# Order alone: a planner that derives each operation's latest time from its own plan, and plans anew, three times

## The chip, the cores and the metric

One core of a Trainium2 chip runs the whole kernel. Time is microseconds (us) on the device, for one launch; smaller is better. The core's engines: TensorE (PE; its weight loads are shown as PEld), VectorE (DVE), ScalarE (ACT), GpSimd (POOL) and SyncE (SP), which here does nothing but issue DMA transfers.

## The reference, cut to what matters

Attention, then a feed-forward block, then a gated MLP, one into the next, all in float32 (the second and third block's weights come in 64 bits and are decoded in the kernel):

```
# B, H, S, D = 4, 12, 448, 64
s = 30 * tanh(q @ k.T / sqrt(D) / 30)                # softcap
x = softmax(s) @ v                                   # -> (4, 448, 768)
xn = (x - mean(x)) / sqrt(var(x) + 1e-6) * g_ln
x = x + relu(xn @ w_ch1) @ w_ch2                     # 768 -> 3072 -> 768
h = relu(x @ w_in)                                   # 768 -> 1024
u, v = h[..., :512], h[..., 512:]
v_s = w_spatial @ norm(v) + b_spatial                # over the 448 positions
out = (u * v_s) @ w_out                              # 512 -> 768
```

## The kernel before

The kernel's code does not issue instructions as it runs. Each call on an engine is *recorded* as an operation of a `Program`: its engine (or two or three alternatives, where `add`, `sub`, `cp` and the like allow several), a cost estimate, what it writes and reads, and the pooled buffers that it uses. A pooled buffer (`Buf`) gets a real tile of its pool (`Slots`) only when its first operation is planned, and gives it back when its last use is done. At the end `issue()` asks `order()` for a list of operations and emits it, so every instruction of the main part stands at one line of the profile, L553 (L588 after the change): one reads it by tile names, not by lines.

`order()` has two parts. The first gives each operation a number `due`. Matmul groups get the sum of the costs of the matmuls recorded ahead of them; everything else is traced backwards from its successors, at `SLACK` (0.35) of the costs in between. The second, `plan(due)`, is a list scheduler. It keeps a clock `now`, and whenever an engine is free it takes, among the engine's ready operations, the one with the smallest `due`, if tiles can be had for it and if that `due` is not further away than `reach()`. Before the change the reach is `spent + AHEAD`: matmul cost spent so far, plus 28. An operation with alternatives goes to its second or third engine only if the first would be later (`BIAS`). The plan decides three things: the order on each engine, which engine does an operation that has alternatives, and which tile a buffer gets.

The work in time. Attention fills about the first 105 us: scores into PSUM (`two`), softcap and exponential on ACT (`es`), with decoding of weights beside them. Decoded weights are stored in DRAM (`kept_w1_*`, `kept_w2_*`) for a second use, since the batch of four is worked in two halves. The feed-forward and gated stages follow in both halves, matmul after matmul. Their products are each three matmuls of a high and a low part (`rs`, `rx`, `rh`: activations; `wh`, `whb`, `whf`, `wab`: weights; a high part is a cast, a low part a subtraction), and blocks of 2x2 are combined in seven products instead of eight, with sums of tiles made on DVE. Hidden tiles of the feed-forward block go to DRAM (`h1_<product>_<tile> <- hs`, `<- hh`) and come back (`hs <- h1_..`). In the second half, kept w1 weights come through `wrb` to `whb`, two early w2 weights through `wr` to `wh`, and later w2 weights through `wq` to `wh`. A w1 or w2 weight serves six output tiles in the stages spoken of here, 3 matmuls each, so 18 matmuls of 448 columns. All transfers go through one queue, SP's, in the order of the plan.

```
cost, latency = 0.5, 4 * out.size() / 360e3      # a transfer, as the planner sees it
cost = 0.14 + n / 960                            # a DVE operation with two inputs
V.scalar_tensor_tensor(out=ti, in0=lo, scalar=29, in1=ti, op0=ALU.logical_shift_right, ...
SP.dma_start(out=kept2[j // KD][:, :, j % KD], in_=t.rearrange("p (a n) -> p a n", a=2))
```

The last two lines are the end of a weight's decoding (`value`): `wc` is the decoded tile, and storing it frees it for the next weight.

Of the kernel before, what the change touches and what calls it, by code (L numbers as in the profile page):

```python
# [44 lines left out]


AHEAD = 28
SLACK = 0.35
BIAS = 0.1
OPEN = 20.0  # L50
# [20 lines left out]
class View:  # L71


    def __init__(self, buf, ap, path=()):
        self.buf, self.at, self.path = buf, ap, path
# [25 lines left out]
class Buf:  # L101
    def __init__(self, pool, name):
        self.pool, self.name = pool, name
        self.first = self.last = None
        self.uses = self.left = 0
        self.tile = None
        self.after = []
        self.gates = []

# [39 lines left out]
class Slots:  # L149
# [19 lines left out]
            b.left, b.tile = b.uses, None  # L169

    def take(self, b):
        b.tile = self.idle.popleft()
        self.held.add(b)
        self.changes += 1

# [43 lines left out]
class Program:  # L219
# [102 lines left out]
    def order(self):  # L322
        n = len(self.ops)
        pred = self.edges()
        self.pred, self.succ = pred, [[] for _ in range(n)]
        for i, ds in enumerate(pred):
            for j, at in ds.items():
                self.succ[j].append((i, at))
        self.bufs = []
        for i, (_, writes, reads) in enumerate(self.ops):  # L330
            mine = list(dict.fromkeys(a.buf for a in chain(writes, reads) if isinstance(a, View)))
            for b in mine:
                b.first = i if b.first is None else b.first
                b.last = i
                b.uses += 1
            self.bufs.append(mine)
        self.pools = {b.pool for m in self.bufs for b in m}
        total = 0.0
        due = [float("inf")] * n
        for i in range(n):  # L340
            engine, cost = self.ops[i][0][0][:2]
            if engine == "PE":
                due[i] = total
                total += cost
            elif i in self.soon:
                due[i] = total
        for p in self.pools:
            p.reuse()
        for s in self.stages:
            begins = [b for p in s.pools for b in p.bufs if b.first is not None]  # L350
            if s.after and begins:
                first = min(begins, key=lambda b: b.first)
                for a in s.after:
                    for b in (b for p in a.pools for b in p.bufs if not b.after):
                        assert b.last < first.first
                        b.gates.append(first)
        for i in reversed(range(n)):
            engine, cost, latency = self.ops[i][0][0][:3]
            latency += 1.4 if engine == "D" else 0.0
            for j, at in chain(self.succ[i], {(a.first, 0.0) for b in self.bufs[i] for a in b.after},  # L360
                               {(a.first, -OPEN / SLACK) for b in self.bufs[i] for a in b.gates}):
                due[i] = min(due[i], due[j] + at * SLACK - (cost + latency + self.DELAY) * SLACK)
            if due[i] == float("inf"):
                due[i] = total
        for i in self.first:
            due[i] = float("-inf")
        return self.plan(due)

    def plan(self, due):

        n = len(self.ops)
        succ, bufs = self.succ, self.bufs
        for p in self.pools:
            p.reset()
# [4 lines left out]
        free = {e: 0.0 for e in self.engines}  # L379
# [5 lines left out]
        spent = moved = 0.0  # L385
        relief = float("-inf")
        blocked = {}

        def release(i):
            for k, alt in enumerate(self.ops[i][0]):  # L390
                heapq.heappush(ready[alt[0]], (due[i], i, k))
# [12 lines left out]
            return False  # L404

        def reach():
            return max(spent + AHEAD, relief)

        def pick(e):


            q = ready[e]
            skipped = []
            found = None
            while q and found is None:
                d, i, k = heapq.heappop(q)
                if taken[i]:
                    continue
                if d > reach():
                    skipped.append((d, i, k))  # L420
                    break
                if k:
                    alt = self.ops[i][0]
                    home = alt[0][0]
                    wait = max(0.0, free[home] - now) if busy[home] else 0.0
                    for d2, i2, k2 in ready[home]:
                        if not taken[i2] and (d2, i2) <= (d, i) and not k2:
                            wait += self.ops[i2][0][0][1]
                    if alt[k][1] > wait + BIAS:
                        skipped.append((d, i, k))  # L430
                        continue
                if not room(i):
                    skipped.append((d, i, k))
                    continue
                found = i, k
            for x in skipped:
                heapq.heappush(q, x)
            return found

        for i in range(n):  # L440
            if not left[i]:
                release(i)
        now = 0.0
        while True:
            for e in ready:
                if busy[e]:
                    continue
                found = pick(e)
                if found is None:
                    continue  # L450
                i, k = found
                taken[i] = True
                out.append((i, k))
                for b in bufs[i]:
                    if b.tile is None:
                        b.pool.take(b)
                busy[e] = True
                cost, latency = self.ops[i][0][k][1:3]
                if e == "PE":
                    spent += cost  # L460
                free[e] = now + cost
                if e == "D":
                    moved = max(moved, now + 1.5) + latency
                    latency = moved + 0.77 - now - cost
                heapq.heappush(events, (now + cost, 0, seq, e))
                done = now + cost + latency + self.DELAY
                for j, at in succ[i]:
                    heapq.heappush(events, (max(now, done - at), 1, seq, j))
                    seq += 1
                heapq.heappush(events, (done, 2, seq, i))  # L470
                seq += 1
            if not events:
                rest = [d for q in ready.values() for d, i, _ in q if not taken[i] and d > reach()]
                if not rest:
                    break
                relief = min(rest)
                continue
            relief = float("-inf")
            now, kind, _, x = heapq.heappop(events)
            if kind == 0:  # L480
                busy[x] = False
            elif kind == 1:
                left[x] -= 1
                if not left[x]:
                    release(x)
            else:
                for b in bufs[x]:
                    b.left -= 1
                    if not b.left:
                        b.pool.give(b)  # L490
                        if b.pool.stage is not None and not b.pool.stage.left:
                            for s in b.pool.stage.then:
                                if not s.open and all(not a.left for a in s.after):
                                    s.open = True
                                    out.append((s, None))
                                    for p in s.pools:
                                        p.changes += 1
        assert sum(k is not None for _, k in out) == n
        return out

# [1342 lines left out]
```

## Time and profile before

| | |
|---|---|
| runs shown | 1015.18, 1011.96, 1010.72 us; median 1011.96 |
| profiled execution | 1010.06 us; its span 1008.3 us, so 1.76 us lie around the span |
| granted TensorE clock | 1.000 over the span |
| TensorE matmul busy | 999.5 us, 99% of the span, 5060 matmuls |
| TensorE weight load busy | 828.4 us, 82% |
| DVE busy | 868.3 us, 86%, 1472 instructions |
| ACT busy | 580.5 us, 58%, 925 instructions |
| POOL busy | 23.0 us, 22 instructions |
| DMA | 229.05 MB, mean 227 GB/s |

An engine's busy time is the sum of its instructions' spans; matmuls overlap, so a busy TensorE is not a TensorE at its peak. What an instruction waited for is told by who released it. The waits of TensorE are what the span consists of beside its matmuls.

### The profile page before, as it was taken

The numbers are of one execution on the slowest core, as the hardware profiler recorded it, in microseconds if no ns is written. First come the engines' busy times: TensorE is split into PE (matmuls) and PEld (weight loads), VectorE is DVE, ScalarE is ACT, GpSimd is POOL, SyncE is SP. The second block draws the span as 40 slices with busy tenths as digits, with TensorE's granted clock in tenths as the row PEclk, the third lists the DMA queues.
The fourth block names the chain that finished last, engine by engine and source line by source line (L and its number), as shares of the span: only waits on it lengthen the run. The fifth ranks groups of instructions, "written<-read, shape, count | busy, mean of one in ns | idle before, by whom it ended". The sixth has DMA issues, their size and how long they took to land.

```text
span 1008.3 us, 14836 instructions
## 1 busy us (share of the span) xinstructions
PE 999.5 (99%) x5060; PEld 828.4 (82%) x5060; DVE 868.3 (86%) x1472; ACT 580.5 (58%) x925; POOL 23.0 (2%) x22
## 2 busy tenths in 40 slices
PE   9999999999999999999999999999999999999998
PEld 2332788778778899999989899999999999998987
DVE  6979898878888789999869999877788988968996
ACT  8999776776667347674335355444454542314653
POOL 0000110000000000000001200000000000000010
PEclk9999999999999999999999999999999999999999
DMA  8444779999999999998044143565699867302402
GB/s 282 136 128 146 261 262 366 357 365 356 343 368 361 362 376 323 330 405 276 26 154 141 39 138 122 176 194 191 232 330 375 291 183 233 103 22 71 128 22 110
DMA packets 124848, 229.05 MB, mean 227 GB/s; under 512 B 21170, under 2 KB 93028, under 8 KB 124772
## 3 DMA queue, kind: packets, MB, share of 16 engines
q1 hardware_dynamic: 124772, 228.10, 66.0%
q8 instruction: 40, 0.66, 0.3%
q14 instruction: 36, 0.29, 0.1%
HBM read 157.48 MB, written 70.57 MB: 226 GB/s over the span
## 4 chain that ended last, share of the span: by engine, by line
PE 78%; DMA 11%; DVE 6%; ACT 3%; issue 1%; SPq 1%; DVEq 0%; ACTq 0%
PE bank L553 51%; PE two L553 26%; DMA hs<-inv 3%; DMA w<-in_w_dram 3%; DVE es L553 2%; DMA kept_w<-wc 2%; DMA rc<-sum 1%; ACT es L553 1%; SPq L553 1%; DMA inv<-rc 1%; DVE wr L553 1%; DVE hs L553 1%; ACT hs L553 1%; DMA qk<-in_qk_dram 1%; DVE x L553 1%
## 5 line engine op out<-in xcount | busy, mean ns | idle before, releaser
L553 PE MATMUL bank<-rs,wh 128*128 128x448 f32 x1728 | 361.9, 363 | 0.3 <-ACT hs L553 0.2
L553 PEld LDWEIGHTS bank<-rs,wh 128*128 128x128 f32 x1728 | 322.8, 187 | 27.5 <-issue 4.3
L553 PE MATMUL two<-rs,wh 128*128 128x448 f32 x462 | 103.4, 362 | 0.0
L553 ACT ACTIVATE rs<-hs 128x448 fp32r<-128x448 f32 x137 | 74.6, 570 | 43.0 <-DMA hs<-h 33.2
L553 DVE TENSOR_TENSOR rs<-hs,rs 128x448 fp32r<-128x448 f32 x159 | 94.2, 618 | 1.8 <-ACT rs L553 1.4
L553 PEld LDWEIGHTS two<-rs,wh 128*128 128x128 f32 x462 | 86.6, 187 | 5.8
L553 ACT ACTIVATE es<-es,capt 128x896 f32<-128x896 f32 x72 | 73.1, 1057 | 0.0
L553 ACT ACTIVATE es<-two,qsc 128x896 f32<-128x896 f32 x62 | 60.7, 1017 | 6.8 <-PE two L553 6.6
L553 PE MATMUL bank<-es,vt 128*64 128x448 f32 x288 | 62.2, 552 | 0.0
L553 DVE TENSOR_TENSOR wh<-wr,wh 128x768 fp32r<-128x768 f32 (+2 forms) x66 | 56.3, 856 | 3.8 <-ACT wh L553 3.5
L553 ACT ACTIVATE hs<-bank 128x448 f32<-128x448 f32 x62 | 33.6, 541 | 44.6 <-PE bank L553 34.5
L553 ACT ACTIVATE wh<-wr 128x768 fp32r<-128x768 f32 (+2 forms) x50 | 38.5, 770 | 28.2 <-PE bank L553 15.3
L553 DVE TENSOR_TENSOR es<-es,es 128x896 f32<-128x896 f32 x48 | 51.9, 1081 | 1.8 <-ACT es L553 1.4
L553 PEld LDWEIGHTS bank<-es,vt 128*64 128x64 f32 x288 | 17.4, 136 | 36.9 <-issue 26.7
L553 PE MATMUL two<-qk 64*128 64x448 f32 x168 | 39.9, 580 | 2.0 <-ACT es L553 2.0
L553 ACT ACTIVATE wc<-w 128x512 f32<-128x512 f32 x36 | 24.2, 674 | 30.0 <-DMA kept_w<-wc 13.3
L553 ACT ACTIVATE rs<-x 128x448 fp32r<-128x448 f32 x32 | 18.0, 574 | 37.5 <-DVE x L553 36.1
L553 PEld LDWEIGHTS two<-qk 64*128 64x128 f32 x168 | 14.1, 190 | 27.3 <-ACT es L553 15.4
L553 PE MATMUL two<-wh,rs 128*128 128x512 f32 x144 | 34.7, 390 | 0.0
L553 PE MATMUL bank<-rx,whb 128*128 128x448 f32 x144 | 32.7, 362 | 0.0
L553 PE MATMUL two<-rx,whb 128*128 128x448 f32 x144 | 32.7, 362 | 0.0
L553 DVE TENSOR_SCALAR wc<-wc 128x512 int32<-128x512 int32 x36 | 15.2, 423 | 19.3 <-ACT wc L553 19.0
(249 smaller groups left out, 1878.9 us busy)
## 6 DMA issues: line engine op xcount, KB each, us to landing
hs<-h SPq DMA_DIRECT2D x168, 224.0 KB, 5.2
h<-hx SPq DMA_DIRECT2D x84, 224.0 KB, 5.3
w<-in_w_dram SPq DMA_DIRECT2D x24, 768.0 KB, 6.8
w<-in_w_dram SPq DMA_DIRECT2D x36, 512.0 KB, 6.4
qk<-in_qk_dram SPq DMA_DIRECT2D x24, 448.0 KB, 5.1
h<-hs SPq DMA_DIRECT2D x48, 224.0 KB, 3.7
kept_w<-wr SPq DMA_DIRECT2D x24, 384.0 KB, 7.6
kept_w<-wc SPq DMA_DIRECT2D x36, 256.0 KB, 5.3
```

Of the source, the lines that this page charges most:

```text
L553: fn(*(put(a) for a in args), **{k: put(a) for k, a in kw.items()})
```

## The change

The formula for `due` is kept as a first guess. With it the planner makes a plan as before. Then `latest()` goes through that plan from its end: an operation's latest time is the earliest of what its engine does next, of its successors, and of the next buffer that gets its tile, each less the lag seen in the plan, and less its cost. These times become the `due` of the next plan; for it, `reach()` is `now + WITHIN` (20), since `due` is now on the plan's own clock. That is done three times (`ROUNDS`); of the four plans the one with the smallest end by the planner's own costs is made again and issued. Nothing that is computed changes, and no operation is added or left out; what changes is order, choice of engine, and tiles.

```diff
+WITHIN = 20
+ROUNDS = 3
...
-        self.tile = None
+        self.tile = self.tile_at = None
...
-        b.tile = self.idle.popleft()
+        b.tile = b.tile_at = self.idle.popleft()
...
-        for i in self.first:
-            due[i] = float("-inf")
-        return self.plan(due)
-
-    def plan(self, due):
+        tries = []
+        for timed in (False,) + (True,) * ROUNDS:
+            for i in self.first:
+                due[i] = float("-inf")
+            plan = self.plan(due, timed)
+            tries.append((self.end, len(tries), due, timed))
+            due = self.latest(plan)
+        _, _, due, timed = min(tries)
+        return self.plan(due, timed)
+
+    def latest(self, plan):
...
+        late = [float("inf")] * len(self.ops)
+        free = {e: self.end for e in self.engines}
+        then = [[] for _ in self.ops]
+        users, holds = {}, {}
+        for i, k in plan:
+            if k is None:
+                continue
+            for b in self.bufs[i]:
+                t = id(b.tile_at)
+                if holds.get(t) is not b:
+                    for j in users.get(t, ()):
+                        then[j].append(i)
+                    holds[t], users[t] = b, []
+                users[t].append(i)
+        for i, k in sorted((x for x in plan if x[1] is not None), key=lambda x: -self.span[x[0]][0]):
+            e, cost = self.ops[i][0][k][:2]
+            lag = self.span[i][1] - self.span[i][0] - cost
+            t = min(chain([free[e]], (late[j] + at - lag for j, at in self.succ[i]), (late[j] - lag for j in then[i])))
+            late[i] = free[e] = t - cost
+        return late
+
+    def plan(self, due, timed):
...
-            return max(spent + AHEAD, relief)
+            return max(now + WITHIN if timed else spent + AHEAD, relief)
...
+                self.span[i] = now, done
...
+        self.end = now
```

TensorE's order is the same before and after, operation for operation. On the other engines operations move. Of those that may go to either engine, 70 casts and copies go from ACT to DVE and 59 from DVE to ACT, 2 operations go from POOL to DVE and 1 from DVE to POOL. The order listing has 1459 rows on DVE before and 1472 after, 927 and 916 on ACT, 27 and 26 on POOL, 833 and 836 on SP; some rows stand for several instructions. Three places follow.

The first is on SP, at the end of attention, before:

```order
L553 DMA vt1_0_423<-in_v_dram 64x2x64
L553 DMA w41_442<-in_w2_dram 128x1024
L553 DMA kept_w2_0_164<-wc1_440 256x1x256
L553 DMA vt1_0_423<-in_v_dram 128x2x192
L553 DMA qk0_420<-in_qk_dram 128x896
L553 DMA h0_1_0_168<-hx0_429 128x448
```

and after:

```order
L588 DMA vt1_0_423<-in_v_dram 64x2x64
L588 DMA w41_442<-in_w2_dram 128x1024
L588 DMA vt1_0_423<-in_v_dram 128x2x192
L588 DMA qk0_420<-in_qk_dram 128x896
L588 DMA kept_w2_0_164<-wc1_440 256x1x256
L588 DMA h0_1_0_168<-hx0_429 128x448
```

`wc0`, `wc1` are decoded w2 weights, `w41` a raw one, `vt1_0` and `qk0` are inputs of the last attention head, `hx0` a hidden tile. The store of `wc1` has moved behind two loads.

The second is on SP, in the second half of the batch, where the feed-forward block goes over from w1 to w2. Before:

```order
L553 DMA hs7_86<-h1_7_2_340 128x448
L553 DMA hs1_80<-h1_7_3_347 128x448
L553 DMA h1_1_11_398<-hh1_5133 128x448
L553 DMA hs4_83<-h1_7_4_354 128x448
L553 DMA wq0_6533<-kept_w2_12_209 128x768
L553 DMA wq1_6534<-kept_w2_18_223 128x768
L553 DMA h1_2_11_400<-hh5_5137 128x448
```

and after:

```order
L588 DMA hs8_87<-h1_7_3_347 128x448
L588 DMA h1_4_10_397<-hs7_86 128x448
L588 DMA hs2_81<-h1_7_4_354 128x448
L588 DMA h1_3_11_399<-hs9_88 128x448
L588 DMA hs5_84<-h1_7_5_361 128x448
L588 DMA hs1_80<-h1_7_6_368 128x448
L588 DMA hs3_82<-h1_7_7_375 128x448
L588 DMA h1_1_11_398<-hh3_5135 128x448
L588 DMA hs7_86<-h1_7_8_382 128x448
L588 DMA wq0_6543<-kept_w2_12_209 128x768
L588 DMA wq1_6544<-kept_w2_18_223 128x768
```

The rows `hs<-h1_7_n` load hidden tiles (operands of the seventh product), `h1_..<-hh` store some, and `wq0` is the first weight of the `wq` group. Ahead of `wq0` stand the loads of `h1_7_2` to `h1_7_4` before, and of `h1_7_2` to `h1_7_8` after: four more. In the same way, going back some 20 rows, the load of `kept_w1_21` to `wrb0` has no load of a `h1_1_n` tile ahead of it before and seven after, and one more of a weight (`kept_w2_6`); its place among the rows goes from 649 to 664.

The third is on DVE, near the end, where gated tiles are multiplied in. Before:

```order
L553 TENSOR_TENSOR x1_1_119<-x1_1_119,hs4_83 128x448
L553 TENSOR_TENSOR x1_2_120<-bank2_139,x0_5_117 128x448
L553 TENSOR_TENSOR hs2_81<-x1_1_119,x0_1_113 128x448
L553 TENSOR_TENSOR rc3_7732<-hs1_80,rc3_7732 128x448
L553 TENSOR_TENSOR x1_3_121<-two0_141,x0_5_117 128x448
L553 TENSOR_TENSOR rc0_7729<-hs2_81,rc0_7729 128x448
```

and after:

```order
L588 TENSOR_TENSOR x1_1_119<-x1_1_119,hs5_84 128x448
L588 TENSOR_TENSOR x1_2_120<-bank0_137,x0_5_117 128x448
L588 TENSOR_TENSOR hs0_79<-x1_1_119,x0_1_113 128x448
L588 TENSOR_TENSOR x1_2_120<-x1_2_120,hs6_85 128x448
L588 TENSOR_TENSOR rc3_7732<-hs4_83,rc3_7732 128x448
L588 TENSOR_TENSOR x1_3_121<-two0_141,x0_5_117 128x448
```

A multiplication that writes `x1_2` in place stands there now, the fourth row. It was POOL's last one, whose end of the list read, before:

```order
L553 TENSOR_TENSOR qkg1_4396<-qkg1_4396,hs9_88 128x448
L553 TENSOR_TENSOR small0_97<-small0_97,mhalf_130 128x4
L553 TENSOR_TENSOR small0_97<-small0_97,mhalf_130 128x3
L553 TENSOR_TENSOR x0_2_114<-x0_2_114,hs2_81 128x448
L553 TENSOR_TENSOR x1_2_120<-x1_2_120,hs0_79 128x448
```

and after:

```order
L588 TENSOR_TENSOR rstd_t1_134<-var_t1_133,mhalf_130 112x4
L588 TENSOR_TENSOR qkg0_4397<-qkg0_4397,hs7_86 128x448
L588 TENSOR_TENSOR small0_97<-small0_97,mhalf_130 128x4
L588 TENSOR_TENSOR small0_97<-small0_97,mhalf_130 128x3
L588 TENSOR_TENSOR x0_2_114<-x0_2_114,hs7_86 128x448
```

## Rows read from the trace of the kernel before

**Rows 1.** The page, part 1: busy us (share of the span) xinstructions, by engine.
```profile
PE 999.5 (99%) x5060; PEld 828.4 (82%) x5060; DVE 868.3 (86%) x1472; ACT 580.5 (58%) x925; POOL 23.0 (2%) x22
```

**Rows 2.** Windows A:B, length; busy us (x) of each engine; PEclk, DMA share, GB/s.
```profile
47.00:98.00 51.00, 49.51 (x240) 15.46 (x236) 45.26 (x78) 49.02 (x67) 0.00 (x0) 1.00 0.47 138
...
113.00:988.00 875.00, 874.70 (x4472) 773.34 (x4473) 761.42 (x1290) 472.67 (x780) 22.19 (x13) 1.00 0.68 235
976.00:991.00 15.00, 14.72 (x71) 12.83 (x69) 14.72 (x28) 8.67 (x18) 1.41 (x1) 1.00 0.00 1
...
350.00:400.00 50.00, 50.00 (x252) 46.86 (x251) 44.89 (x69) 27.84 (x46) 0.00 (x0) 1.00 1.03 369
...
750.00:765.00 15.00, 15.00 (x77) 14.06 (x76) 11.77 (x21) 7.10 (x12) 0.00 (x0) 1.00 0.96 314
```

**Rows 3.** What TensorE waited for: total us, times, longest.
```profile
PE two L553 <- ACT es L553: 2.0, 3, 1.0
...
PE bank L553 <- DVE wh L553: 0.6, 2, 0.4
```

**Rows 4.** Timeline of ACT near 47: start us, us, line, op, out<-in, xcount.
```profile
47.63 0.54 ACT L553 ACTIVATE hs<-bank 128x448 f32<-128x448 f32 x1
```

**Rows 5.** The chain of waits that ended last, from 98 to 124: start us, us, what.
```profile
105.00 5.63 DMA kept_w<-wc
...
110.74 0.66 ACT wc L553
111.40 0.44 ACT hx L553
...
112.34 0.64 DVE wh L553
...
113.02 4.49 PE bank L553 x21
```

**Rows 6.** Timeline of SP, which issues the transfers, near 105.
```profile
105.61 0.60 SPq L553 DMA_DIRECT2D vt<-in_v_dram  x1
106.25 0.66 SPq L553 DMA_DIRECT2D qk<-in_qk_dram  x1
```

**Rows 7.** Timeline of SP in the FFN's second half.
```profile
727.01 0.39 SPq L553 DMA_DIRECT2D wrb<-kept_w  x1
...
751.44 0.92 SPq L553 DMA_DIRECT2D hs<-h  x2
754.61 0.32 SPq L553 DMA_DIRECT2D h<-hh  x1
...
755.51 0.89 SPq L553 DMA_DIRECT2D wq<-kept_w  x2
```

**Rows 8.** Timeline of ACT there: casts of a kept weight.
```profile
736.98 0.85 ACT L553 ACTIVATE whb<-wrb 128x768 fp32r<-128x768 f32 x1 [0.69 <-ACT wab L553]
...
760.17 0.85 ACT L553 ACTIVATE wh<-wq 128x768 fp32r<-128x768 f32 x1 [1.09 <-DMA wq<-kept_w]
```

**Rows 9.** Timeline of DVE there: the low half of the same weights.
```profile
737.86 0.96 DVE L553 TENSOR_TENSOR whb<-wrb,whb 128x768 fp32r<-128x768 f32 x1 [0.29 <-ACT whb L553]
...
761.05 0.96 DVE L553 TENSOR_TENSOR wh<-wq,wh 128x768 fp32r<-128x768 f32 x1 [0.36 <-ACT wh L553]
```

**Rows 10.** Timeline of TensorE there.
```profile
740.53 0.76 PE L553 MATMUL bank<-rs,whb 128*128 128x448 f32 x3
...
754.95 15.36 PE L553 MATMUL bank<-rs,wh 128*128 128x448 f32 x76
```

**Rows 11.** Timeline of POOL near the end.
```profile
976.93 1.41 POOL L553 TENSOR_TENSOR x<-x,hs 128x448 f32<-128x448 f32 x1 [5.14 <-DVE x L553]
```

**Rows 12.** Timeline of DVE there.
```profile
977.23 1.58 DVE L553 TENSOR_TENSOR rc<-hs,rc 128x448 fp32r<-128x448 f32 x1
...
979.27 0.61 DVE L553 TENSOR_TENSOR rc<-hs,rc 128x448 fp32r<-128x448 f32 x1
```

**Rows 13.** The chain of waits, from 970 to the end.
```profile
990.70 0.54 DVE rc L553
```

More of the change, by code (lines that the diff above doesn't have):

```diff
@@ L364, in order @@
                 due[i] = total
-        for i in self.first:
-            due[i] = float("-inf")
-        return self.plan(due)
-    def plan(self, due):
+        tries = []
[29 more added lines that the diff above has]
+    def plan(self, due, timed):
         n = len(self.ops)
+        self.span = [None] * n
         succ, bufs = self.succ, self.bufs
@@ L438, in pick @@
             return found
+        now = 0.0
         for i in range(n):
@@ L442, in plan @@
                 release(i)
-        now = 0.0
         while True:
```

## Prediction

> **What bounds the kernel now.** I read the page's busy shares first, then the table of windows, then the waits of TensorE, and last the chain of waits at the places where order changes.
>
> TensorE is busy 999.5 of 1008.3 us [rows 1]. That alone could mislead, because matmuls overlap. The windows say where it is true. From 350 to 400 it does 252 matmuls in 50 us, 0.198 us each; from 113 to 988 it is busy for 874.70 of 875.00 us, and its weight loads for 773.34 [rows 2]. Nothing is to be won there by order: a new order can only leave it so, or break it. From 47 to 98 things are different. TensorE still shows 49.51 of 51.00 us, but its weight loads only 15.46; ACT shows 49.02 of 51.00 [rows 2]. So ACT sets the pace there. Near the end, from 976 to 991, DVE is busy for 14.72 of 15.00 us [rows 2], and the chain of waits runs through it up to the last block of matmuls [rows 13]. The granted clock is 1.00 in all these windows [rows 2], the upper of its two levels, so the clock has nothing to give back.
>
> The waits of TensorE confirm it: the largest group is 2.0 us for exponentials, in three pieces, and weights on DVE cost 0.6 us in two [rows 3]. All of these are small against the 5.06 us (0.5% of 1011.96) that a measurement of this kernel can tell from no change.
>
> **The change, part by part.** TensorE's own order is the same operation for operation. DVE is idle for 1008.3 - 868.3 = 140 us of the span and ACT for 1008.3 - 580.5 = 428 us [rows 1]. So the 129 casts and copies that change sides between ACT and DVE, net 11 to DVE (11 x 0.55 = 6 us by rows like the copy in [rows 4]), are costed at nothing where neither engine is full: from 113 to 988 DVE has 875.00 - 761.42 = 113.6 us idle, ACT 402.3 [rows 2]. If that cover were gone, each would cost its 0.4 to 0.9 us on the path; the tight stretches, 47 to 98 and 976 to 991, are costed by themselves below. What is left is five places.
>
> *The copy at 47.6.* In the ACT-bound stretch one copy out of PSUM, 0.54 us [rows 4], goes from ACT to DVE, which has 51.00 - 45.26 = 5.7 us idle there [rows 2]. Gain between 0 (if TensorE sets the next step anyway) and 0.54. I take the middle: **-0.3**.
>
> *The store at 105.* The only chain around attention's end that waits for a transfer runs through it. The store of `kept_w<-wc` is issued at 105.00 and takes 5.63 us; ACT decodes the next weight into the freed tile at 110.74, ends the activations that follow it, DVE makes the weight's low half at 112.34, and TensorE goes on at 113.02 [rows 5]. After the change two loads stand ahead of the store on SP, 0.60 and 0.66 us to issue [rows 6]. It starts 1.26 us later, so does ACT. One thing comes back: the eviction `hx`, 0.44 us in the chain behind ACT's decoding [rows 5], now stands ahead of the decoding in ACT's order and runs while it waits. 1.26 - 0.44 = **+0.8**. Below it is 0 (if the store lands sooner after its issue by as much as it is issued later), above 1.26.
>
> *The w1 weights near 730.* The load of `kept_w1_21` has seven loads of hidden tiles and one of a weight ahead of it that it did not have. A hidden tile is 128 x 448 x 4 = 229 KB, a weight of 128 x 768 is 393 KB; at the 314 GB/s of the window at 750 [rows 2] that is 0.73 and 1.25 us, together 7 x 0.73 + 1.25 = 6.4 us. Slack against it: before, the load is issued at 727.01 [rows 7] and takes 0.39 us to issue, but its cast only comes at 736.98 [rows 8]. The low half ends at 737.86 + 0.96 = 738.82 [rows 9], and TensorE wants it at 740.53 [rows 10]: 1.7 us more. If the ten us from issue to cast absorb nothing, the price is 6.4 - 1.7 = 4.7; if they absorb it, nothing. Since the weight was ready long before its cast, I stay near the lower end: **+0.3**.
>
> *The first `wq` weight at 755.* Four loads of hidden tiles more stand ahead of it, 4 x 0.73 = 2.9 us of transfer. Before, it is issued at 755.51 [rows 7] and cast on ACT at 760.17, right when it lands [rows 8]; the low half ends at 761.05 + 0.96 = 762.01 [rows 9]. TensorE needs it after 36 matmuls of the two earlier weights, at 754.95 + 36 x 0.198 = 762.08 [rows 10]. So the margin is 0.1 us. In the new order the cast goes to DVE, which in this stretch does such a cast in 0.56 us instead of ACT's 0.85 [rows 8]: 0.3 back, 0.4 us of margin in all. Above, the loss is 2.9 - 0.4 = 2.5. But SP is not issuing from 751.44 + 0.92 = 752.36 to 754.61 [rows 7]: it waits for hidden tiles to be stored. Four issues at some 0.46 us (0.92 for two) are 1.8 us, and fit in that gap where tiles are free. I take a delay of 0.8, so a wait of 0.8 - 0.4 = **+0.4**.
>
> A rule bears on this one. The Trainium skill, "DMA: Bandwidth & Descriptors", section "Queues, rings and completion order", says that each DMA engine takes the descriptors of a ring in the order they were put in. By that rule nothing queued ahead is overtaken, and the place costs its upper end, 2.5 us instead of 0.4, whenever the DMA engines are full. The window at 750 shows a DMA share of 0.96 [rows 2], which is nearly full.
>
> *The multiplication at 977.* POOL's last one takes 1.41 us from 976.93 [rows 11]. Beside it DVE's operation at 977.23 takes 1.58 us; the same shape at 979.27, with POOL idle, takes 0.61 [rows 12]. On DVE the multiplication costs about 0.54 us (its neighbours start 0.53 to 0.54 us apart), and the 0.97 us of stretching goes. DVE is full there, and the last matmuls wait for its end at 990.70 + 0.54 [rows 13]. So -0.97 + 0.54 = **-0.4**. Bounds: 0, if ACT's part of the chain takes over, and -0.97.
>
> Sum: -0.3 + 0.8 + 0.3 + 0.4 - 0.4 = **+0.8 us**. On the profiled execution, 1008.3 + 0.8 + 1.76 around the span = 1010.9. That execution lies 1.9 us under the median of the runs shown; on the median the sum gives 1011.96 + 0.8 = **1012.8**. Both signs are within what cannot be told from no change. With every bound at its worse end it is 0 + 1.26 + 4.7 + 2.5 - 0 = +8.5, with every one at its better end -0.54 + 0 + 0 + 0 - 0.97 = -1.5.
>
> **The rivals.**
>
> *Hidden tiles crowd out the weights, slower.* The second half of the feed-forward block is where DMA is fullest, and the new order brings loads of hidden tiles forward that TensorE wants only later. If a load queued ahead costs its full transfer time at both places, the sum is -0.3 + 0.8 + 4.7 + 2.5 - 0.4 = +7.3: 1019.3. It decides (more than 5.06) from about eight of the eleven tiles on, if none is hidden in the gaps of SP. For it: the DMA share of 0.96, the margin of 0.1 us. Against it: the gap at 752.36, and ten us between issue and cast at 727. Chance 0.13.
>
> *The first 113 us come into order, faster.* TensorE's 99% could hide room: from 47 to 98 its weight loads are busy for 30% (15.46 of 51.00), against 88% (773.34 of 875.00) later [rows 2]. A better order of ACT and DVE could win there. But ACT itself is idle for 51.00 - 49.02 = 2.0 us only, and one operation leaves it: 2.0 + 0.54, with both weight waits of 0.6 [rows 3] and the 0.97 at 977, makes 4.1 us at most, 1007.9 on the median. To be over 5.06 the waits before 47 would have to go as well. The order on ACT and DVE there hardly changes, which speaks against. Chance 0.04.
>
> The Trainium skill, "Perfetto Trace Analysis", section "Identifying the Most-Contended Engine", says that matmul busy share is a poor measure of how near TensorE is to its limit, and that weight load busy share is better. By that measure, the page's 82% would leave 18% open. The row of the windows agrees for attention, and the row of ACT says that the room isn't TensorE's own to take.
>
> *The change does nothing.* TensorE's order, the tight resource, is untouched, and all that moves could sit in slack: 1012.0, within 0.3. The moved store at 105, in a chain without slack, speaks against it being exactly nothing. Chance 0.07.
>
> **How the numbers follow.** My forecast, small waits added and small ones removed, has 0.76; its own range is 1010 to 1016 (-1.5 to +4). With doing nothing at 0.07 and a hundredth of the forecast's own tail beyond 5.06 added to the slower rival, the chances are: faster 0.04, same 0.82, slower 0.14. The range takes in the lower bound of the sum and the spread of the runs' median, which lie 1.2 under and 3.2 over, and most of the way to the slower rival: **1009.0 to 1018.0**; about 0.1 is left out on each side.
>
> **What would show it.** In the changed profile: TensorE's wait for a DVE weight near 113 grows from 0.2 or 0.4 to about 1 us, with the store of `wc` issued near 106.3. A wait for `wh` of up to 1 us near 762, none or little near 740. POOL has one row less near 977, and no DVE row of 1.58 us beside it. TensorE's busy time from 113 to 988 stays within 1 us of its length. I am wrong if TensorE waits for weights for several us between 725 and 765, if the stretch 47 to 98 shortens by more than 2 us, or if a wait shows at a place not named here, where an operation was pulled back to its latest time and then came later than planned.

## The result, and the profile after

The changed kernel takes 1020.69 us (median of 6 runs, 1019.88 to 1024.08), the kernel before 1012.22 (6 runs, 1010.72 to 1016.43): ratio 1.0086, 95% interval 1.0068 to 1.0105. It is slower by some 8.5 us, outside the range of 1009.0 to 1018.0. The profiled execution took 1019.88 us, its span 1018.1, which is 9.8 more than before.

The page of the changed kernel, part 1, answers to [rows 1]:

```profile
PE 1002.8 (98%) x5060; PEld 830.4 (82%) x5060; DVE 873.3 (86%) x1484; ACT 575.6 (57%) x914; POOL 17.9 (2%) x21
```

and what TensorE waited for, in the whole span, to [rows 3]:

```profile
PE bank L588 <- DVE hs L588: 3.2, 2, 2.0
PE two L588 <- ACT es L588: 3.1, 3, 2.1
PE bank L588 <- ACT wh L588: 2.0, 1, 2.0
PE bank L1820 <- DVE x L1818: 1.4, 1, 1.4
PE bank L588 <- ACT hs L588: 1.3, 2, 0.8
PE bank L588 <- DVE rc L588: 0.3, 1, 0.3
PE two L588 <- ACT hs L588: 0.2, 1, 0.2
```

These are 11.5 us, against 4.9 before: 6.6 more. TensorE's busy time, which counts overlapping matmuls once, is 3.3 us more, for the same 5060 matmuls. 6.6 + 3.3 = 9.9 is the whole difference of the spans. The second term is the clock. The table of windows of the changed kernel shows the granted clock at its lower level (0.50, 1.2 GHz) behind two of the waits of 2 us, those for `wh` and `hs`, where in the kernel before it is 1.00 throughout:

```profile
112.00:114.00 2.00, 0.07 (x1) 0.07 (x1) 0.52 (x2) 1.25 (x3) 0.00 (x0) 0.95 1.03 429
114.00:116.00 2.00, 2.00 (x5) 1.50 (x6) 2.00 (x3) 1.43 (x3) 0.00 (x0) 0.50 1.01 400
116.00:118.00 2.00, 2.00 (x9) 1.81 (x8) 1.97 (x4) 0.00 (x0) 0.00 (x0) 0.69 0.94 314
...
328.00:330.00 2.00, 1.10 (x3) 1.01 (x4) 1.01 (x3) 0.00 (x0) 0.00 (x0) 0.71 1.04 397
330.00:332.00 2.00, 2.00 (x7) 1.78 (x6) 1.07 (x3) 1.46 (x2) 0.00 (x0) 0.50 1.03 395
```

Since TensorE's order is the same, the start of the n-th matmul can be compared in the two traces. That says where the time went:

```
matmul number        440     460     520     1240    1460    1680    1700    3700    4740    5000
start before, us    96.66  102.03  114.53  244.13  283.82  323.14  327.14  728.93  940.35  992.40
start after, us     94.76  101.31  117.32  247.72  287.73  332.06  336.17  737.80  950.25 1002.02
after - before      -1.90   -0.71   +2.79   +3.60   +3.91   +8.91   +9.03   +8.87   +9.89   +9.62
```

4.7 us (from -1.90 to +2.79) are lost from 95 to 117, 6.2 from there to 336, and 0.6 after that. From 400 to 990, where the prediction saw two dangerous places, TensorE does not wait for more than 0.2 us.

The two larger places look alike. The chain of waits of the changed kernel near 113 (as [rows 5]):

```profile
105.12 7.53 DMA kept_w<-wc
...
112.75 0.66 ACT wc L588
113.41 0.47 ACT wh L588
...
113.93 6.37 PE bank L588 x22
```

and the timeline of DVE near 328, followed by TensorE's:

```profile
328.13 0.24 DVE L588 RECIPROCAL rc<-rc 128x14 f32<-128x14 f32 x1 [2.69 <-DMA rc<-sum]
328.29 0.56 DVE L588 COPY hs<-bank 128x448 f32<-128x448 f32 x1
```

```profile
328.90 1.49 PE L588 MATMUL bank<-rs,wh 128*128 128x448 f32 x3 [1.98 <-DVE hs L588]
```

In both, an operation that waits for a transfer (a decoding into the tile `wc`, whose store has to land first; a reciprocal of sums that come back from DRAM) stands on its engine directly ahead of one that TensorE wants (the cast `wh`; the eviction `hs<-bank`). I first took this to be the whole cause, place by place; the experiments say otherwise.

### The profile page after: what moved, and what is told of

The parts are those of the page before. It is cut to its first block, busy times and chain, and to the rows that moved or that the text cites. A ratio compares the mean times of both kernels' runs of the same rounds, so it can differ in the third digit from the quotient of the medians.

```text
span 1018.1 us, 14868 instructions
## 1 busy us (share of the span) xinstructions
PE 1002.8 (98%) x5060; PEld 830.4 (82%) x5060; DVE 873.3 (86%) x1484; ACT 575.6 (57%) x914; POOL 17.9 (2%) x21
## 4 chain that ended last, share of the span: by engine, by line
PE 75%; DMA 12%; DVE 6%; ACT 4%; issue 1%; SPq 1%; ACTq 0%; DVEq 0%
PE bank L588 48%; PE two L588 27%; DMA kept_w<-wc 4%; DMA w<-in_w_dram 3%; ACT es L588 2%; DMA h<-hx 2%; DVE es L588 1%; DMA rc<-sum 1%; SPq L588 1%; ACT hs L588 1%; DVE hs L588 1%; DVE wr L588 1%; DVE rs L588 1%; DMA hs<-inv 1%; DMA hs<-std 1%
## 5 line engine op out<-in xcount | busy, mean ns | idle before, releaser
L588 ACT ACTIVATE rs<-hs 128x448 fp32r<-128x448 f32 x132 | 72.4, 570 | 26.5 <-DMA hs<-h 24.3
L588 PEld LDWEIGHTS bank<-es,vt 128*64 128x64 f32 x288 | 17.4, 136 | 36.9 <-issue 27.4
L588 ACT ACTIVATE wh<-wr 128x768 fp32r<-128x768 f32 (+2 forms) x43 | 33.5, 779 | 22.2 <-DVE wr L588 10.7
```

Of the source, the lines that this page charges most:

```text
L588: fn(*(put(a) for a in args), **{k: put(a) for k, a in kw.items()})
```

## The experiments

All ratios are to the kernel before, in runs on the same chip. Each edit moves operations in the finished plan, or changes who issues or what is stored; all else of the plan stays, unless said.

**1. Mending single places.** Theory H: each place costs by itself. The edits take an operation (or some) out of the plan's list and put it back behind another:

```diff
+MOVES = (((1209, 1210), 1292),)                # a_rc: reciprocal and its store behind hs<-bank, near 328
+MOVES = (((549,), 408), ((550,), 409))         # a_wh: decoding of wc behind the cast wh, near 113
+MOVES = (((492,), 548),)                       # a_store: the store near 105 ahead of two loads again
+MOVES = (((933, 934), 969), ((1122, 1123, 1170), 1206))   # a_two: the like near 246 and 305
```

> The changed kernel with two operations moved: near 328 the reciprocal on DVE that waits for the transfer rc<-sum (and the store of its result) is issued behind the copy hs<-bank, not ahead of it. Theory H (an operation that waits for a transfer stands ahead, on its engine, of one that TensorE wants): TensorE's 1.98 us wait near 328 goes, and with it the fall of the granted clock to 0.5 behind it (1.7 us): -3.7 us against the changed kernel's 1020.7, so 1017.0, ratio to before 1.005. Theory Q (the order of transfers on the queue is what is worse, and TensorE waits for data that land late anyway) and theory S (DVE has been given too much work, so the copy is late by DVE's own load): within 0.7 us of the changed kernel, ratio 1.008 to 1.009.

> The changed kernel with the decoding of the next weight on ACT (wc<-w, which waits for the store of the tile's old content) issued behind the cast wh<-acc near 113, and its second step on DVE behind the low half. Theory H: the cast is done at about 109.6, TensorE's 2.05 us wait at 113.9 goes and the clock does not fall behind it (1.7 us): -3.7, 1017.0, ratio 1.005. Theory Q: the store lands as late as before (112.7), the next weight is late by as much, and TensorE waits a little later instead: within 1 us of 1020.7. The prediction's own term would have it at -0.8.

> The changed kernel with the one move on the queue undone that the prediction costed at +0.8: the store kept_w2<-wc near 105 is issued ahead of the loads of vt and qk again. The prediction: -0.8, 1019.9. Theory Q: it lands 5.6 us after its issue as in the kernel before, near 109.8, so ACT is not late and TensorE's wait of 2.05 and the clock's fall of 1.7 go: -3.7, 1017.0. Theory H, which leaves ACT's order as it is: the store starts 1.0 earlier but is still crowded by the loads of w that stand behind it in the new order, so the landing comes about 1.0 earlier: -1.0 for the wait, and the clock's fall only shortens: -1 to -2.5.

> The changed kernel with two places mended at once: near 246 ACT's decoding wc<-w (waits for a store) and its second step behind the copy hs<-bank; near 305 two decoding steps on DVE, and the load into the tile that they free, behind the copy hs<-bank. Theory H: TensorE's waits of 0.8 near 246 and 1.2 near 306 go: -2.0, 1018.7, ratio 1.0065. Theories Q and S: no change, 1020.7, or slower by what the later load costs.

Measured: a_rc 1023.38 (ratio 1.0100, 1.0071 to 1.0129), a_wh 1020.23 (1.0078, 1.0053 to 1.0104), a_store 1020.55 (1.0080, 1.0053 to 1.0106), a_two 1021.61 (1.0098, 1.0062 to 1.0134). None is faster than the changed kernel beyond its interval. Yet at its own place each of the first three did what H says: from matmul 500 to 520 a_wh and a_store start 4.0 us less late than the changed kernel, from 1660 to 1680 a_rc 3.4 less. The time was given back further on. In a_two the wait of 0.8 near 246 went too, and one of 1.7 us near 287 came. In a_rc the next 20 matmuls lose 5.35. Its timeline of ACT, then of TensorE, shows to what:

```profile
332.44 0.66 ACT L595 ACTIVATE wc<-w 128x512 f32<-128x512 f32 x1 [4.43 <-DMA kept_w<-wc]
...
334.39 1.00 ACT L595 ACTIVATE es<-two,qsc 128x896 f32<-128x896 f32 x1
```

```profile
335.98 6.26 PE L595 MATMUL bank<-rs,wh 128*128 128x448 f32 x22 [4.12 <-ACT es L595]
```

The next decoding waits for its store, and this time the evictions `es<-two` stand behind it.

**2. All four places of H at once, and the transfers.** Theory D: from 150 to 340 the transfers are the bound.

```diff
# a_all: the moves of a_rc, a_wh and a_two together
# a_rel, b_rel (changed kernel, kernel before): every odd w1 weight is not stored, its neighbour is loaded
+                d = kept[kind, j - 1]
...
+                if kind == "w1" and j % 2:
+                    prog.add("D", 0.5, 4 * d.size() / 360e3, lambda: None, [d], [t])
# b_load: the kernel before, five transfers more
+    for i in (769, 849, 937, 1014, 1102):
+        prog.more[i] = partial(nc.sync.dma_start, out=dram.tile([128, 2 * S], F32, name=f"more_{i}"),
+                               in_=qk[0, 0:2].rearrange("a p n -> (a p) n")[64:192])
```

> The changed kernel with all four mends of single places together (near 113 and 246 on ACT, near 305 and 328 on DVE). Theory H (each place costs by itself): the waits of 2.05, 0.8, 1.2 and 2.0 and two falls of the clock of 1.7 each go, -9.4, so about 1011.3, ratio 0.999. Theory D (from 150 to 340 the transfers are the bound: their share is 1.0 there, so time won at one place is waited for at the next): only what is won ahead of 150 can count, and that is caught up in the full stretch too: 1017 to 1021, ratio 1.005 to 1.009.

> The changed kernel, same plan, with 12 of the 24 stores of decoded w1 weights left out (every odd one, 0.393 MB each, 4.7 MB; the second half loads its even neighbour in its place, so the output isn't the reference's). Theory D: the full stretch is relieved, TensorE's waits from 240 to 335 and their clock fall (6 us of the 9.8) go, what was lost near 113 (about 3) stays: 1014 to 1015. Theory H: the operations that stand ahead of those TensorE wants are still there, and the landings they wait for are little earlier: 1018 or more.

> The kernel before with the same 12 stores left out (same output remark). Theory D says the kernel before just meets the limit of the transfers (no TensorE wait from 120 to 990): 1010 to 1013, no change. The control for the run on the changed kernel: if this one gains as much as that, the relief has nothing to do with the change.

> The kernel before, same plan, with five transfers more, DRAM to DRAM, 0.459 MB each (2.29 MB), issued on SP behind the loads of five w1 weights from 155 to 239; nothing waits for them. Theory D (transfers at their limit from 150 to 340): 2.29 MB at 361 GB/s are 6.4 us that nothing absorbs, 1016 to 1019, with TensorE's waits between 200 and 340. If TensorE alone is the bound there, as the prediction has it, the queue has room: within 1.5 us of the kernel before.

Measured: a_all 1022.86 (1.0107, 1.0072 to 1.0142), a_rel 1013.29 (1.0010, 0.9988 to 1.0032), b_rel 1010.79 (0.9980, 0.9962 to 0.9997), b_load 1014.53 (1.0030, 1.0009 to 1.0052). H as a sum of places has fallen: with all four mended nothing is won, and one wait of 4.4 us for `es` takes their place. Leaving out 4.7 MB of stores takes 1020.69 - 1013.29 = 7.4 us from the changed kernel and 1012.62 - 1010.79 = 1.8 from the one before. That is D's forecast and a little more, since the wait near 113 goes too. b_load is between its two forecasts: of 6.4 us of transfer time added (2.29 MB at 361 GB/s), about 2 appear. So the kernel before is near the limit, with some 4 us of room, not at it.

The windows from 150 to 340; the kernel before, then the changed one:

```profile
150.00:340.00 190.00, 189.72 (x1056) 147.86 (x1055) 157.43 (x252) 130.13 (x185) 1.04 (x1) 1.00 1.01 361
```

```profile
150.00:340.00 190.00, 185.55 (x1023) 145.84 (x1022) 153.38 (x248) 125.94 (x180) 0.00 (x0) 0.99 1.00 351
```

The share of the transfer engines is 1.01 and 1.00, but 361 and 351 GB/s were moved. 10 GB/s over 190 us are 1.9 MB, which at 361 GB/s take 5.3 us: nearly the 6.2 lost in the stretch. The same bytes in a longer time would show so too; the rates alone don't say which is the cause. One difference is at the head of the queue. Adding up the rows of SP's waits from 150 to 340, those ended by an engine are 20.3 us in 48 before and 27.5 us in 55 after, and those ended by a transfer 54.9 and 46.0. And ACT, from 100 to 340, the kernel before and the changed one:

```profile
ACT wc L553 <- DMA kept_w<-wc: 13.3, 10, 3.1
```

```profile
ACT wc L588 <- DMA kept_w<-wc: 29.8, 15, 4.3
```

**3. The same plan, with the stores taken off the queue; and the reach.**

```diff
# a_pool, b_pool: the stores of decoded weights, all else as it was
+    def store(o, a):
+        prog.add("D", 0.5, 4 * o.size() / 360e3, lambda: nc.gpsimd.dma_start(out=o, in_=a.place()), [o], [a])
...
-                SP.dma_start(out=d, in_=t)
+                store(d, t)
# a_w40, a_w12: another plan
-WITHIN = 20
+WITHIN = 40   (12)
-        _, _, due, timed = min(tries)
+        _, _, due, timed = tries[1]
```

> The changed kernel, same plan, with the 75 stores of decoded weights (kept_w) issued by POOL, which is nearly idle, in place of SP. Theory D in the form that the queue is what falls short (SP's head waits for an engine's result, 27.5 us from 150 to 340 against 20.3 in the kernel before, and the transfers behind it stand still): SP no longer waits for decodings, moves over 355 GB/s from 150 to 340 in place of 351, and the time falls to 1012 to 1016. Rival: the 16 transfer engines themselves are full (share 1.00), whoever issues: 1019 to 1022. Slower than that if POOL's issuing takes DVE's time.

> The kernel before with the same stores issued by POOL; the control. Where SP's head is the limit, the kernel before gains little, since TensorE does not wait there: 1010 to 1013. If issuing from POOL costs by itself (beside DVE), it shows here: over 1014.

> The changed planner with the first plan by latest times always issued and its reach at now + 40 in place of now + 20, so transfers may be issued further ahead. If the short reach leaves the transfers idle from 120 to 150 (share 0.56 against 0.68 before) and so starts the full stretch late, the share there rises to 0.65 or more and the time falls to 1012 to 1016. If it is the order by latest times as such that puts operations that wait for a transfer ahead of those that TensorE wants, 1018 to 1025 as with 20.

> The same with the reach at now + 12. If the reach decides: share from 120 to 150 at 0.5 or less, and over 1024. If the order by latest times decides: 1018 to 1025. A shorter reach also keeps operations closer to the kernel before (mean move on SP's queue 2.0 places, against 3.6 with 20 and 6.3 with 40): if distance from the old order decides, this one is the fastest of the three, 1014 to 1017, and 40 the slowest.

Measured: a_pool 1011.78 (1.0004, 0.9985 to 1.0023), b_pool 1011.18 (0.9985, 0.9972 to 0.9998), a_w40 1031.04 (1.0161, 1.0113 to 1.0209), a_w12 1022.29 (1.0090, 1.0060 to 1.0121). (The trace has 76 such stores, 60 of w1 and w2 and 16 of the gated block.) This is the clearest result: the plan that costs 8.5 us costs nothing measurable if its stores of weights are issued by POOL. Its windows row, and what TensorE waited for in the whole span (three waits of 0.2 us each left out):

```profile
150.00:340.00 190.00, 190.00 (x1059) 148.24 (x1058) 160.66 (x260) 127.81 (x183) 28.51 (x44) 1.00 1.00 364
```

```profile
PE two L588 <- ACT es L588: 3.1, 3, 2.1
PE bank L1823 <- DVE x L1821: 1.4, 1, 1.4
PE bank L588 <- DVE rc L588: 0.3, 1, 0.3
```

TensorE does not wait at all in the stretch, 364 GB/s are moved with the same busy share of 1.00, and ACT's wait for `kept_w<-wc` is down from 29.8 to 0.4 us:

```profile
ACT wc L588 <- DMA kept_w<-wc: 0.4, 1, 0.4
```

The bytes of the stores are not the cost, as a_rel alone would allow: here all of them are moved. The time and the rate came as D forecast, the reason did not: SP's head waits longer for engines in a_pool than in the changed kernel, 35.5 us in 57 pieces (45.6 in b_pool), and in the five kernels of 1 and 2 with mended places it waits 23.4 to 25.6 us without any gain. So the total of SP's head waits does not measure the loss. ACT's waits for transfers go with it better: from 100 to 340 they are 33.3 us in the kernel before, 51.5 in the changed one, 41.3 to 57.1 in the five, 14.0 in a_pool. They are no measure for every plan: a_w40, slower than all of these, has 27.4. In a_pool it is POOL that stands waiting for decodings, from 150 to 340:

```profile
POOL kept_w L749 <- DVE wc L588: 97.0, 22, 12.0
POOL kept_w L749 <- DVE wr L588: 61.8, 18, 13.0
```

The reach does not explain the loss: with 40 the share from 120 to 150 is 0.58, not 0.65, and the time is longest; with 12, closest to the old order, the share is 0.65 and the time still 1022.

**4. By which way the stores cost.** Theory W: ACT waits for one of two `wc` tiles. Against D.

```diff
# a_wc3, b_wc3: three tiles of 512 in turn for two of 768; orders unchanged
+                        seen[b] = b.tile = idle.popleft()
...
+    wc.size, prog.wide = 2, wc
# a_soon: each store kept_w<-wc right behind the operation that makes its content
# b_late: the kernel before, each of them four places later on SP
```

> The changed kernel, same order on every engine, with three tiles for wc in turn in place of two (each 512 wide in place of 768, the same memory). Theory W (ACT stands waiting for a store to land before it decodes into a wc tile, and casts and evictions that TensorE wants stand behind it): ACT's wait for kept_w<-wc from 100 to 340 falls from 29.8 to under 8 us and the time to 1012 to 1014. Theory D (the queue moves less because SP's head waits for engines): the queue's order and its waits for engines are the same, so 1018 to 1021.

> The same third tile in the kernel before, the control. Both theories: ACT's waits for kept_w<-wc (13.3 us) go too, but TensorE does not wait behind them: 1010 to 1013.

> The changed kernel with each of the 36 stores kept_w<-wc issued on SP right behind the operation that makes its content (on average 4 transfers stood in between). Theory W: the tiles come free sooner, ACT waits less for them: 1014 to 1018. Theory D: SP's head now waits longer for DVE (the store is issued before its content is ready), and the queue moves less: 1020 to 1026.

> The kernel before with each of these stores four places later on SP (fewer for four of the last). Theory W: about 2 us later landing per tile, ACT's wait for kept_w<-wc rises from 13 to 30 us or more, and TensorE waits behind it as in the changed kernel: 1017 to 1025. Theory D: SP's head waits less for DVE: 1010 to 1013.

Measured: a_wc3 1018.79 (1.0058, 1.0037 to 1.0080), b_wc3 1012.12 (0.9990, 0.9975 to 1.0005), a_soon 1018.68 (1.0052, 1.0032 to 1.0072), b_late 1035.25 (1.0220, 1.0186 to 1.0255). Neither theory alone holds. In a_wc3 ACT no longer waits for the store, but it waits as long for the load of the raw weight. Here is one decoding near 310, in the changed kernel and then in a_wc3:

```profile
310.92 0.66 ACT L588 ACTIVATE wc<-w 128x512 f32<-128x512 f32 x1 [4.26 <-DMA kept_w<-wc]
```

```profile
310.75 0.67 ACT L602 ACTIVATE wc<-w 128x512 f32<-128x512 f32 x1 [4.28 <-DMA w<-in_w_dram]
```

ACT's waits for any transfer from 100 to 340 add up to 51.5 us in the changed kernel and 47.7 in a_wc3. W had the wait for the store going and the time with it, to 1012 to 1014; the wait went, the time hardly moved. D forecast no loss for b_late, W one to 1025 at most, and it is the slowest of all: ACT waits 55.2 us for `kept_w<-wc` alone, in 22 pieces, SP's head waits 58.0 us for engines, and 329 GB/s are moved.

```profile
ACT wc L560 <- DMA kept_w<-wc: 55.2, 22, 5.6
```

I read the two as one loop. A store that is late holds up ACT; what ACT does late, SP's head waits for; and all transfers behind that head, the next raw weight among them, come later. b_late shows that late stores cost, and a_pool that the loss needs the stores in SP's queue; the links between are argued from the waits, not tested one by one. Stores earlier on SP (a_soon) recover about 2 us, less than POOL's issuing.

**5. The engines' shares, and the prediction's own term.**

```diff
# a_eng: the changed kernel's order, each operation on the engine that it had before
+        plan = [(i, ENGINE.get(i, k)) for i, k in plan]
# b_st: the kernel before, the loads of vt and qk ahead of the store near 105
+MOVES = (((477, 474), 548),)
```

> The changed kernel with its order, but every one of the 132 operations that changed sides on the engine that it had before. Theory S (the shift from ACT to DVE is the cost): the loss goes, 1012 to 1015. If order and transfers are the cost: 1018 to 1023, since ACT, which already waits 51.5 us for transfers from 100 to 340, gets its work back.

> The kernel before with the two loads of vt and qk issued ahead of the store kept_w<-wc near 105, as in the changed kernel, and nothing else moved. The prediction's term: +0.8 (0 to 1.26), so 1013.4, and TensorE's wait near 113 grows from 0.2 to about 1. If the later landing is as in the changed kernel (7.5 us after the issue in place of 5.6) TensorE waits about 2 there and the clock falls: +2 to +4, and in the full stretch behind it this may be kept or grow, 1014.5 to 1017.

Measured: a_eng 1025.80 (1.0125, 1.0097 to 1.0153), b_st 1015.42 (1.0035, 1.0016 to 1.0054). The shift of casts to DVE is not the cost in the new order: without it that order is no faster, and a_eng is slower than both theories had it. (The new engines in the old order were not run.) In b_st the median is 3.7 us up, but not for the prediction's reason. Its chain of waits:

```profile
104.95 6.50 DMA kept_w<-wc
...
111.56 0.67 ACT wc L560
...
113.83 4.28 PE bank L560 x20
```

TensorE goes on 0.81 us later than in [rows 5], 113.83 for 113.02. That it is the forecast +0.8 is chance: TensorE was 0.76 late already at matmul 460 (102.79 for 102.03), ahead of the store, and it waits no longer here than before. The kernel before, then b_st:

```profile
113.02 0.47 PE L553 MATMUL bank<-wh,onesr 128*128 128x448 f32 x1 [0.19 <-DVE wh L553]
```

```profile
113.83 0.47 PE L560 MATMUL bank<-wh,onesr 128*128 128x448 f32 x1 [0.19 <-DVE wh L560]
```

So the place costs 0.05 us. The store was not issued later either (104.95 for 105.00); it took 0.87 longer. The end is 5.4 us later in that profile, and the larger part comes near 436, where TensorE waits 0.55 and 1.05 us for `whm`, a later weight, and the clock falls to 0.68 from 436 to 440. I have no run that ties this second loss to the moved store.

## Why the prediction was wrong

**The step that failed** is the costing of everything between 113 and 720 at nothing: what changes there is "costed at nothing where neither engine is full", since DVE and ACT have idle time [rows 2], and "what is left is five places". That the casts changed sides is not what costs (a_eng); that the order around them changed does, and with the stores off SP's queue it does not (a_pool). Idle time of an engine is cover only if the engine can use it. Of ACT's time from 100 to 340, 33.3 us were spent waiting for transfers in the kernel before, with everything behind held up in order. The prediction weighed the transfers only near 755, where their share is 0.96, and not from 150 to 340, where it is 1.01; the row of 350 to 400 in [rows 2], read for its matmuls alone, shows 1.03. The 6.2 us of that stretch had no term. The last sign of being wrong that the prediction gave, a wait at a place not named, came near 246, 306 and 328 (0.8, 1.2 and 2.0 us). That "a new order can only leave it so, or break it" was right, and it broke.

**The store at 105**: right place, wrong step, too small. The prediction took a later issue (1.26 us) and assumed the same 5.63 us to land. In the changed kernel the store was issued at 105.12, about as before, but took 7.53. Two loads stood ahead of it, and two loads of 768 KB were now issued from 107.2 on. In b_st, with the first two alone, it took 6.50, so about half of the 1.9 us more goes with them; the rest I put down to the other two, which no run shows by itself. The reordered eviction gave its 0.44 back: in the chain the cast follows the decoding directly. TensorE's wait of 2.05 us then brought the clock down, to a mean of 0.95, 0.50 and 0.69 in the three windows of 2 us from 112 to 118, so 0.1 + 1.0 + 0.6 = 1.7 us more. The term of +0.8 measured 3.5 from matmul 460 to 520. In the kernel before, with nothing else moved, it is 0.05 at the place (b_st).

**The w1 weights near 730 and the `wq` weight at 755**, +0.3 and +0.4, and the slower rival built on them: TensorE shows no wait over 0.15 us for them. Matmuls 1700 to 3700 lose nothing. Of 0.4 us between 3700 and 3750 none is for a weight: TensorE's weight loads wait 0.3 and 0.2 us there for the evictions `hh` and `hs`. At the first `wq` weight 0.13 us are lost. It was issued at 764.70 for 755.51, no later than before with TensorE 9.25 us behind; its cast came at 770.20 for 760.17, 0.8 later, the delay that the prediction took, though from the landing and not from the issue. The Trainium skill's rule on the order of a ring ("DMA: Bandwidth & Descriptors", "Queues, rings and completion order") would have put the place at 2.5 us, by the prediction's working; no run here shows that price there. The rival's general idea, data that come late on a full queue, fits what happened 400 us earlier, but no run shows hidden tiles crowding out weights there.

**The multiplication at 977**, -0.4: confirmed, a little smaller. DVE now does it in 0.62 us at 987.17, the operation behind it takes 0.62 instead of the 1.58 of [rows 12], and from matmul 4740 to 5000 0.27 us are gained:

```profile
987.17 0.62 DVE L588 TENSOR_TENSOR x<-x,hs 128x448 f32<-128x448 f32 x1
987.71 0.62 DVE L588 TENSOR_TENSOR rc<-hs,rc 128x448 fp32r<-128x448 f32 x1
```

**The copy at 47.6**, -0.3: matmul 440 starts 1.9 us earlier, but 1.2 of that are lost by 460 in a wait for `es` of 2.1 us, and the profiles of six other kernels with the same order up to here start matmul 440 anywhere from 1.4 us earlier to 0.5 later than the kernel before. Not settled. The faster rival saw nothing: TensorE's total wait for `es` went from 2.0 to 3.1.

**What stays open.** POOL's issuing does several things at once: the stores no longer stand in SP's queue, SP is spared issuing them (0.55 us each for `kept_w<-wc`, 0.42 for `kept_w<-wr`, medians), they go through a queue of another kind (the page of a_pool lists 23.60 MB as software_dynamic), and more transfers can be under way. No run here takes these apart. Nor did I find the rule of the planner that makes the plan worse; three different plans by latest times (reach 12, 20, 40) cost 9, 8.5 and 18 us, so it isn't the one number.

## What to carry to other kernels

Here TensorE was busy at 99% beside transfers at a share of 1.0, with some 4 us of room between them: an order that kept TensorE's sequence unchanged still lost there, and a mended wait reappeared at the next tight place. Before calling an engine's idle time cover, add up how much of it is waiting for transfers at the head of an in-order queue. And if a plan is bad, test who issues before re-planning: taking 76 stores off the one queue made a plan that was 8.5 us slower take as long as the old one (ratio 1.0004, 0.9985 to 1.0023).

## What the runs showed of the hardware

Two waits of TensorE of 2 us in the changed kernel (2.05 near 113, 1.98 near 328) cost nearly twice their length, because the granted clock stood at 0.50 in the window of 2 us behind each and was back at 1.00 only 3 to 4 us after its end; waits of 0.8 and 1.2 us in the same profile left it at 1.00. The length of the wait alone doesn't decide it. In the same profile a wait of 2.14 us for `es` left the clock at 1.00, and in a_pool the same wait at the same matmul was followed by 0.50. The changed kernel, then a_pool:

```profile
97.44 1.02 PE L588 MATMUL two<-qk 64*128 64x448 f32 x4 [2.14 <-ACT es L588]
...
100.00:102.00 2.00, 2.00 (x12) 1.23 (x9) 0.90 (x3) 2.00 (x5) 0.00 (x0) 1.00 0.67 209
```

```profile
98.86 1.02 PE L588 MATMUL two<-qk 64*128 64x448 f32 x4 [2.15 <-ACT es L588]
...
100.00:102.00 2.00, 2.00 (x6) 0.57 (x6) 1.56 (x3) 2.00 (x3) 0.74 (x2) 0.50 0.67 168
```

From matmul 440 to 460 that costs a_pool 1.7 us more than the changed kernel. So two profiles can differ by that much for one such fall.

A busy share of 0.99 to 1.02 of the transfer engines went with anything from 340 (a_rel) to 368 GB/s (b_load), so the share alone doesn't say that they move what they can.
